# Order of a layer's superblocks, start of the output layer's weight tiles, start of a weight conversion, and the padding of the slots, in a three-layer kernel on one core

## The chip, the cores and the metric

The kernel runs on one core of a Trainium2 chip. The metric is the device time of one execution in microseconds (us); lower is better. The engines are TensorE (PE; PEld is its weight load), VectorE (DVE), ScalarE (ACT), GpSimd (POOL) and SyncE (SP). GpSimd and SyncE also issue DMAs: GpSimd's go through the software queue (q0), SyncE's through the hardware queue (q1).

## What is computed

```python
x = chunk_attention(q, k, v)          # (8, 8, 576, 64), softmax within chunks of 64 positions
x = x.transpose(0, 2, 1, 3).reshape(4608, 512)
h = x @ w_in                          # 512 x 2048
g = np.where(h > 0, h, np.exp(np.minimum(h, 0)) - 1)
y = g @ w_out                         # 2048 x 512
gate = 1 / (1 + np.exp(-(y @ w_gate)))  # 512 x 1536
out = (gate * (y @ w_val)) @ w_out2   # 1536 x 512, result 4608 x 512
```

The weights come as 64-bit floating-point words, which the kernel itself turns into pairs of a high and a low part.

## The kernel before

**Arithmetic.** Every factor is split into a high and a low part, and every product is three matmul passes (`PASSES`: high by high, low by high, high by low). The second layer, the gate and value layer and the output layer each replace the 8 block products of a 2x2 block product by 7, with sums on VectorE before and after (`PRODUCTS`, the order in which the four PSUM banks x, w, y, z take the 7 products).

**Stages on TensorE.** Stage 1 (0 to 504 us) is the attention (L463, L505) and the first layer (L395). Stage 2 (504 to 853 us) is the second layer (L721): five superblocks of token columns, four of 512 columns per half ("wide") and one, number 4, of 256 ("narrow"). The tuple `ORDER` (L51) says in which order they run. One superblock is 7 products of 48 matmuls. Stage 3 (853 to 1399 us) is the gate and value layer (L859, `unit`): 30 units `n`, six for each superblock in the order 0 to 4, so that units 24 to 29 are narrow; a unit is 7 products of 12 matmuls. Stage 4 (1399 to 1679 us) is the output layer (L990): 9 groups of 7 products of 36 matmuls.

**Weight tiles.** Converted weights lie in DRAM, in tiles of 0.5 MB (`wd_mid` for the second layer, `wd_glu` for gate and value, `wd_out` for the output). A pool `w` of 28 slots holds them in SBUF, together with the split operands of the products (`four`) and the tiles that a conversion works on. `hold(at, room, ahead)` (L320 to L339) is called after each product. It looks up the next `ahead` tiles from place `at` in the list `uses`, fetches those that are not held (L337, a DMA that GpSimd issues), and gives up the tiles used last if more than `room` are held. `uses` (L314 to L317) is the list of all products' tiles in order of time. A superblock of stage 2 uses 28 tiles; `room` is 20 without a conversion running and 12 with one, so that more or fewer tiles survive from one superblock to the next. Group 0 of stage 4 needs 21 `wd_out` tiles, three for each product, and the later groups use the same 21. GpSimd issues in program order: a load that waits for its slot holds up what stands behind it.

**Conversions.** `convert_pairs` (L196) loads raw words (`craw`, L209), puts its steps on ScalarE and VectorE in a list `todo`, from which `bg(n)` runs `n`, and stores the result (L290). The gate and value weights are converted in stage 2 (set up at L838), the output weights in stage 3 (set up at L1041; their raw words are loaded on SyncE's queue).

**Results of a unit.** A unit sums in `s` and `t` (two of ten 8 KB slots: `get`, `free`; a freed slot is given to the next `get` in order of freeing). ScalarE's sigmoids are L876, its first copy from PSUM is L878. `finish` (L912) multiplies gate by value (L914, L916) and stores the halves to DRAM (`gv<-s` L915, `gv<-t` L917, both on SyncE), then frees the slots. It runs after the second product of the next unit. For unit 28 (every sixth less two) the two multiplications are on GpSimd, so they stand in the same instruction stream as the weight loads. Four loads `c<-gv` (L934) bring the first group of stage 4 back; they stand on SyncE among the stores of units 25 to 28. SyncE issues in program order as well.

**Slots.** The ten 8 KB slots lie on two sides of SBUF, 6 right and 4 left. On the right side a tile `pad` (L87) of 8 words (32 bytes per partition) lies ahead of the pools of the right side. With it the right slots, the tiles `three` and stage 1's `x_r` start 64 bytes past a multiple of 128, while the left slots and the `w` pool start on multiples of 128. Where a slot holds `xc` (stage 3's first three operands) or `gc` (24 of the 36 weights of each product of stage 4), TensorE reads it.

Of the kernel before, what the change touches and what calls it, by code (L numbers as in the profile page):

```python
# [8 lines left out]
F32 = mybir.dt.float32  # L9
# [38 lines left out]
NLS = (512, 512, 512, 512, 256)  # L48
NJ = len(NLS)
START = tuple(2 * sum(NLS[:j]) for j in range(NJ))  # L50
ORDER = (0, 1, 2, 4, 3)  # L51
QU = F2 // 2
QM = F1 // 4
PAIRS_1, PAIRS_2 = 17, HF + 2 * QU
# [6 lines left out]
def kernel(  # L61
# [22 lines left out]
    x_l = pa.enter_context(tc.tile_pool(name="x_l", bufs=1))  # L84
    e_p = pa.enter_context(tc.tile_pool(name="e", bufs=4))
    pad_p = ctx.enter_context(tc.tile_pool(name="pad", bufs=1, side="right"))
    pad_p.tile([128, 8], F32, name="pad")  # L87
    pb = ExitStack()
    x_r = pb.enter_context(tc.tile_pool(name="x_r", bufs=1, side="right"))
    ps_p = ctx.enter_context(tc.tile_pool(name="ps", bufs=1, space=bass.MemoryType.PSUM))  # L90
# [15 lines left out]
    todo = []  # L106
# [206 lines left out]
    uses = [("mid", r, i) for _ in range(NJ) for i in range(7) for r in range(QM)]  # L313
    MID = len(uses)  # L314
    seq = [(j, q if j % 2 == 0 else QU - 1 - q) for j in range(NJ) for q in range(QU)]
    uses += [("glu", q, i) for _, q in seq for i in range(7)]
    uses += [("out2", r, i) for i in range(7) for r in range(QU // 2)]  # L317
    held = {}

    def hold(at, room, ahead):  # L320

        soon = {}
        for n, k in enumerate(uses[at:]):
            soon.setdefault(k, n)
        for k in list(held):
            if k not in soon:
                del held[k]
        need = list(soon)[:min(ahead, room)]
        for k in need:
            if not made(k):  # L330
                break
            if k not in held:
                while len(held) >= room:
                    del held[max(held, key=soon.get)]
                m, q, i = k
                t = held[k] = w_p.tile([128, 2, 2, 256], F32R, tag="w", name="w")
                nc.gpsimd.dma_start(out=t, in_=wd[m][q][:, (RIGHT if m == "out2" else LEFT)[i]])  # L337
        while len(held) > room:
            del held[max(held, key=soon.get)]  # L339
# [298 lines left out]
    def room(*busy):  # L638
        return NW - sum(busy)
# [44 lines left out]
    def stage_2(one):  # L684
# [137 lines left out]
        for o, j in enumerate(ORDER):  # L822
            nxt = ORDER[o + 1] if o + 1 < NJ else None
            for i in range(7):
                for p in range(QM):
                    product(j, i, p)
                    if o == i == p == 0:
                        one(end, False)
                        pa.close()
                        open_slots("left", 4)  # L830
                        three_p = ctx.enter_context(
                            tc.tile_pool(name="three", bufs=3, side="right", reuse_waits="tile")
                        )
                    beside(j, nxt, i, p)
                    if nxt is None:
                        for f in first_x.get((i, p), ()):
                            f()
                    if (o, i, p) == (1, 0, 0):  # L838
                        hold(7 * QM, room(8, 8), 10)
                        convert_pairs(range(PAIRS_1, PAIRS_2), nc.gpsimd)  # L840
                    if i in (2, 3, 5) and p > 0 and o > 0:
                        bg(2)
                    last = nxt is None and i >= 4
                    hold((7 * o + i) * QM + p + 1, room(8, 8 if todo or last else 0), 10)
                after(j, i)
# [4 lines left out]
    def unit(n):  # L850
        j, q = seq[n]
        last, third = n % QU == QU - 1, n % QU == QU - 3
        for i, c in enumerate(PRODUCTS):
            ps = bank[c][:, :, 0:NLS[j]]
            w = held["glu", q, i]
            for b in range(2):
                for k in range(2):
                    for p, (zw, zx) in enumerate(PASSES):
                        nc.tensor.matmul(  # L859
                            out=ps[:, b],  # L860
                            lhsT=w[:, b, zw, 128 * k:128 * k + 128],
                            rhs=x_part(j, i, zx, k),
                            start=(i < 4 and k == 0 and p == 0),
                            stop=(k == 1 and p == 2),
                            skip_group_check=True,
                        )
            if last:
                drop_x(j, i)
            parts = 8 if n + 1 < len(seq) else 2 * (7 - max(i, XC - 1))
            hold(MID + 7 * n + i + 1, room(parts, 9 if todo else 0), 14 if n < len(seq) - 3 else 22)  # L870
            if i == 0:
                s, t = get("s", (2, 2, NLS[j])), get("t", (2, 2, NLS[j]))
                u, v, c12 = s[:, 0], s[:, 1], t[:, 0]

                def sigmoid(x, of=None):
                    nc.scalar.activation(out=x, in_=x if of is None else of, func=ACTF.Sigmoid)  # L876

                nc.scalar.copy(out=u, in_=ps)  # L878
            elif i == 1:
                add(u, ps, u)  # L880
                while pending:
                    pending.pop(0)()
            elif i == 2:
                add(v, ps, u)
            elif i == 3:
                add(v, ps, v)
                sigmoid(v[:, 0])
            elif i == 4:
                sigmoid(t[:, 1, 0], ps[:, 0])
                nc.vector.tensor_tensor(out=t[:, 1, 0], in0=ps[:, 1], in1=t[:, 1, 0], op=ALU.mult)  # L890
            elif i == 5:
                add(c12, ps, u)
                sigmoid(c12[:, 0])
            else:
                add(u, ps, u)
                sigmoid(u[:, 0])
            if not last and not third:
                bg(1)
            if j + 1 < NJ:
                if n % QU == 1 and i >= 5:  # L900
                    load_x(j + 1, i - 5)
                if third and 1 <= i <= 3:
                    sum_x(j + 1, i)
                if last:
                    if i == 5:
                        sum_x(j + 1, 4)
                    split_x(j + 1, i)
                    if i == 6:
                        done_x(j + 1)
            yield  # L910

        def finish():  # L912
            eng = nc.gpsimd if n % QU == QU - 2 else nc.vector
            eng.tensor_tensor(out=s[:, :, 0], in0=s[:, :, 1], in1=s[:, :, 0], op=ALU.mult)  # L914
            nc.sync.dma_start(out=gvd[j][:, 0:2, q], in_=s[:, :, 0])  # L915
            eng.tensor_tensor(out=c12[:, 0], in0=c12[:, 1], in1=c12[:, 0], op=ALU.mult)  # L916
            nc.sync.dma_start(out=gvd[j][:, 2:4, q], in_=t[:, :, 0])  # L917
            free(s)
            free(t)
        pending.append(finish)  # L920

    def stages_3_4():
# [77 lines left out]
        def after(g, i):  # L1000
            if i == 0:
                ut[g] = four(2, 256)
                ot[g] = [four(2, DM) for h in range(2)]
            u, (lo, hi) = ut[g], ot[g]
            left, right = slice(0, 256), slice(256, 512)

            def store(h):
                j, k = groups[g]
                for n in range(2):
                    r = START[j] + h * NLS[j] + 256 * k + 128 * n  # L1010
                    nc.sync.dma_start(out=out[r:r + 128, :], in_=ot[g][h][:, n])

            if i == 0:
                nc.scalar.copy(out=u, in_=po["x"])
            elif i == 1:
                add(u, po["w"], u)
            elif i == 2:
                add(hi[:, :, right], po["y"], u)
            elif i == 3:
                add(hi[:, :, right], po["z"], hi[:, :, right])  # L1020
            elif i == 4:
                nc.scalar.copy(out=lo[:, :, left], in_=po["x"])
            elif i == 5:
                add(lo[:, :, right], po["y"], u)
                store(0)
            else:
                add(hi[:, :, left], po["z"], u)
                store(1)
                del ut[g], ot[g]

        N = len(seq)
# [6 lines left out]
            (N - 1, 5): lambda: split_g(0, 0, "c11", keep=True),  # L1038
        }
        for n in range(N):  # L1040
            if n == 2:  # L1041
                hold(MID + 7 * n, room(8, 9), 11)
                convert_pairs(range(PAIRS_2, len(tiles_of)), nc.sync)
            for i, _ in enumerate(unit(n)):
                beside.get((n, i), lambda: None)()
        for g in range(G):
            for i in range(7):
                prepare(g, i)
                product(g, i)
                after(g, i)  # L1050
                while pending:
                    pending.pop(0)()

# [63 lines left out]
```

## Time and profile before

| | us |
|---|---|
| runs shown, median of 3 | 1682.78 |
| lowest and highest of them | 1680.6, 1683.73 |
| the profiled execution, its own time | 1680.64 |
| its span, first to last instruction | 1678.9 |
| PE busy in the span | 1624.6 (97%) |
| DVE busy | 1205.5 (72%) |
| ACT busy | 752.4 (45%) |
| POOL busy | 308.9 (18%) |
| mean granted clock of TensorE | 0.991 of full speed |

A span is the profiled execution of one core; 1.7 us of the execution's time lie around it. In the rows below, "a<-b" is an operation that writes tile a from tile b, "xN" a count, and "<- X" names what ended a wait. A chain is the path that ended last in a stretch, piece by piece.

### The profile page before, as it was taken

What the parts mean: (1) busy time and instruction counts of PE and PEld (TensorE: products, weight loads), DVE (VectorE), ACT (ScalarE), POOL (GpSimd) and SP (SyncE); (2) the same over time, 40 slices, a digit from 0 to 9 for tenths busy, and PEclk for the clock granted to TensorE, in tenths of its full rate; (3) what the DMA queues carried; (4) which work ended last, traced back from release to release, by engine and by line L of the source; (5) the groups of instructions that cost most, each with busy time, mean ns of one, the idle gap of its engine ahead of it and who ended that gap; (6) DMA issues with size and microseconds to landing.
All of it is one profiled execution on the core that took longest, in us unless ns stands there. A gap on an engine that the chain in (4) does not pass through costs nothing.

```text
span 1678.9 us, 27430 instructions
## 1 busy us (share of the span) xinstructions
PE 1624.6 (97%) x10644; PEld 1385.7 (83%) x10644; DVE 1205.5 (72%) x1703; ACT 752.4 (45%) x1277; POOL 308.9 (18%) x502
## 2 busy tenths in 40 slices
PE   6899999999999999999999999999999977999998
PEld 4677777777788888898887888888888977999998
DVE  7878888888547898877945676766744626777776
ACT  5766767666544465545512332422312213333342
POOL 3421122211101122221121222222220230000000
PEclk9999999999999999999999999999999998999999
DMA  6679889898789799998799679699492696443431
GB/s 223 201 238 295 279 286 296 293 293 280 259 290 320 268 301 378 300 362 293 210 322 316 198 248 390 201 342 334 128 403 90 236 390 201 145 158 113 157 132 51
DMA packets 178433, 429.10 MB, mean 256 GB/s; under 512 B 14208, under 2 KB 55168, under 8 KB 173184
## 3 DMA queue, kind: packets, MB, share of 16 engines
q0 software_dynamic: 73344, 223.90, 40.3%
q1 hardware_dynamic: 104960, 203.45, 35.3%
q8 instruction: 84, 1.38, 0.3%
q14 instruction: 45, 0.37, 0.1%
HBM read 294.65 MB, written 132.64 MB: 255 GB/s over the span
## 4 chain that ended last, share of the span: by engine, by line
PE 72%; DVE 12%; ACT 6%; DMA 6%; issue 2%; SPq 1%; POOL 0%; ACTq 0%; DVEq 0%; POOLq 0%
PE bank_x L859 8%; PE bank_y L859 8%; PE bank_z L859 8%; PE bank_y L721 6%; PE bank_z L721 6%; PE bank_x L721 6%; PE bank_x L990 5%; PE bank_z L990 4%; PE bank_w L859 4%; PE bank_y L395 4%; PE bank_w L395 3%; PE bank_z L395 3%; PE bank_w L721 3%; PE bank_y L990 3%; PE bank_w L990 2%
## 5 line engine op out<-in xcount | busy, mean ns | idle before, releaser
L95 ACT CAST four<-b 128x512 fp32r<-128x512 f32 (+1 forms) x240 | 129.1, 576 | 81.4 <-PE bank_y L721 30.9
L101 DVE TENSOR_TENSOR four<-b,four 128x512 fp32r<-128x512 f32 (+1 forms) x240 | 141.3, 632 | 33.3 <-ACT four L95 32.5
L859 PE MATMUL bank_z<-four,w 128*128 128x512 f32 (+1 forms) x720 | 158.5, 369 | 0.0
L876 ACT ACTIVATE s<-s 128x512 f32<-128x512 f32 (+1 forms) x60 | 35.4, 590 | 250.4 <-DVE s L104 250.4
L859 PEld LDWEIGHTS bank_z<-four,w 128*128 128x128 f32 x720 | 126.3, 189 | 23.4
L395 PE MATMUL bank_w<-xs,w 128*128 128x512 f32 x576 | 141.0, 399 | 0.0
L395 PE MATMUL bank_y<-xs,w 128*128 128x512 f32 x576 | 138.9, 395 | 1.4 <-POOL w L167 0.9
L337 POOL DMA_DIRECT2D w<-wd_glu x172 | 92.7, 543 | 255.9 <-PE bank_x L859 68.6
L395 PE MATMUL bank_z<-xs,w 128*128 128x512 f32 x576 | 138.9, 396 | 0.0
L395 PEld LDWEIGHTS bank_y<-xs,w 128*128 128x128 f32 x576 | 106.5, 188 | 23.6 <-POOL w L167 1.2
L395 PEld LDWEIGHTS bank_w<-xs,w 128*128 128x128 f32 x576 | 107.2, 190 | 22.2
L395 PEld LDWEIGHTS bank_z<-xs,w 128*128 128x128 f32 x576 | 107.2, 189 | 22.2
L721 PE MATMUL bank_y<-four,w 128*128 128x512 f32 (+1 forms) x480 | 100.7, 368 | 3.2 <-DMA w<-wd_mid 2.6
L337 POOL DMA_DIRECT2D w<-wd_mid x102 | 54.4, 537 | 267.1 <-DVE four L101 58.2
L721 PE MATMUL bank_x<-four,w 128*128 128x512 f32 (+1 forms) x480 | 100.2, 368 | 0.0
L721 PE MATMUL bank_z<-four,w 128*128 128x512 f32 (+1 forms) x480 | 100.2, 368 | 0.0
L721 PEld LDWEIGHTS bank_y<-four,w 128*128 128x128 f32 x480 | 83.8, 188 | 18.6 <-issue 2.5
L721 PEld LDWEIGHTS bank_x<-four,w 128*128 128x128 f32 x480 | 83.8, 189 | 15.0
L721 PEld LDWEIGHTS bank_z<-four,w 128*128 128x128 f32 x480 | 83.8, 189 | 14.9
L104 DVE TENSOR_TENSOR s<-bank_z,s 128x1024 f32<-128x1024 f32 (+1 forms) x60 | 66.9, 1115 | 37.6 <-PE bank_z L859 37.2
L104 DVE TENSOR_TENSOR s<-bank_w,s 128x1024 f32<-128x1024 f32 (+1 forms) x30 | 33.5, 1116 | 83.9 <-PE bank_w L859 45.3
L859 PE MATMUL bank_x<-four,w 128*128 128x512 f32 (+1 forms) x360 | 80.1, 373 | 10.3 <-ACT s L878 10.3
(165 smaller groups left out, 3321.4 us busy)
## 6 DMA issues: line engine op xcount, KB each, us to landing
w<-wd_glu POOLq DMA_DIRECT2D x172, 512.0 KB, 8.6
w<-wd_mid POOLq DMA_DIRECT2D x102, 512.0 KB, 6.9
gd<-elu SPq DMA_DIRECT2D x72, 512.0 KB, 3.8
b<-gd SPq DMA_DIRECT2D x32, 1024.0 KB, 9.0
c<-gv SPq DMA_DIRECT2D x36, 768.0 KB, 5.2
wd_glu<-ch POOLq DMA_DIRECT2D x36, 512.0 KB, 4.8
raw<-in_qkv SPq DMA_DIRECT2D x61, 256.0 KB, 3.9
wd_mid<-ch POOLq DMA_DIRECT2D x24, 512.0 KB, 5.0
```

The costliest lines, as they stand in the source:

```text
L95: nc.scalar.copy(out=out, in_=raw)
L101: lo_eng.tensor_sub(out=lo, in0=raw, in1=hi)
L104: nc.vector.tensor_tensor(out=out, in0=a, in1=b, op=ALU.add)
L337: nc.gpsimd.dma_start(out=t, in_=wd[m][q][:, (RIGHT if m == "out2" else LEFT)[i]])
L395: nc.tensor.matmul(out=h_bank(d)[:, n], lhsT=w[:, zw, kk * 128:(kk + 1) * 128], rhs=xs[j, kk][:, zx], start=(kk == 0 and p == 0), stop=(kk ...
L721: nc.tensor.matmul(out=bank[PRODUCTS[i]][:, u, 0:NLS[j]], lhsT=w[:, k, zw, 128 * u:128 * u + 128], rhs=t[:, zx], start=(i < 4 and p == 0 a ...
L859: nc.tensor.matmul(out=ps[:, b], lhsT=w[:, b, zw, 128 * k:128 * k + 128], rhs=x_part(j, i, zx, k), start=(i < 4 and k == 0 and p == 0), st ...
L876: nc.scalar.activation(out=x, in_=x if of is None else of, func=ACTF.Sigmoid)
L990: nc.tensor.matmul(out=po[c][:, m], lhsT=t[:, zx, q % 4, 128 * m:128 * m + 128], rhs=w[:, q % 2, zw], start=(i < 4 and q == 0 and p == 0 a ...
```

## The change

The edits are all in the order or place of work; the arithmetic is untouched.

```diff
-ORDER = (0, 1, 2, 4, 3)
+ORDER = (0, 4, 1, 2, 3)
...
-    pad_p.tile([128, 8], F32, name="pad")
+    pad_p.tile([128, 24], F32, name="pad")
...
-    uses += [("out2", r, i) for i in range(7) for r in range(QU // 2)]
+    uses += 2 * [("out2", r, i) for i in range(7) for r in range(QU // 2)]
...
-                    if (o, i, p) == (1, 0, 0):
-                        hold(7 * QM, room(8, 8), 10)
+                    if (o, i, p) == (2, 0, 0):
+                        hold(14 * QM, room(8, 8), 10)
                         convert_pairs(range(PAIRS_1, PAIRS_2), nc.gpsimd)
-                    if i in (2, 3, 5) and p > 0 and o > 0:
+                    if i in (2, 3, 5) and p > 0 and o > 1:
                         bg(2)
...
-            hold(MID + 7 * n + i + 1, room(parts, 9 if todo else 0), 14 if n < len(seq) - 3 else 22)
+            hold(MID + 7 * n + i + 1, room(parts, 9 if todo else 0), 14 if n < len(seq) - QU else 10)
...
-            if not last and not third:
+            if not last and not third and n > 1:
                 bg(1)
...
-            if n == 2:
+            if n == 1:
                 hold(MID + 7 * n, room(8, 9), 11)
                 convert_pairs(range(PAIRS_2, len(tiles_of)), nc.sync)
...
                 after(g, i)
+                if g == 0:
+                    hold(MID + 7 * N + 3 * (i + 1), room(7), 10 if i < 4 else 21)
```

Stage 2's narrow superblock runs second instead of fourth, and the conversion of the gate and value weights, which stood beside superblocks 1 and 2, stands beside the same two in their new places. On TensorE this is the only difference (`bank_x` to `bank_z` are the four PSUM banks):

```order
 L721 MATMUL bank_z<-four,w 128x512 x48
+L721 MATMUL bank_x<-four,w 128x256 x48
+L721 MATMUL bank_w<-four,w 128x256 x48
+L721 MATMUL bank_y<-four,w 128x256 x48
+L721 MATMUL bank_z<-four,w 128x256 x48
+L721 MATMUL bank_x<-four,w 128x256 x48
```

These are the first five of the seven narrow products (256 columns), now right behind the first wide superblock; the same seven rows are gone between the fourth and the fifth superblock of the other order.

On SyncE at the start of stage 3, `craw<-in_w_out` are the first raw words of the output's weights, `gv` the stores of a unit and `x` the loads of the next superblock's operand:

```order
 L738 DMA ymid_69<-u 128x1024
+L209 DMA craw<-in_w_out 128x1024 x2
 L915 DMA gv_71<-s 128x2x512
 L917 DMA gv_71<-t 128x2x512
 L646 DMA x<-ymid_67 128x1024 x4
-L209 DMA craw<-in_w_out 128x1024 x2
 L915 DMA gv_71<-s 128x2x512
```

The two raw loads moved from behind unit 0's stores and the four loads of `x` to ahead of them.

On GpSimd at the end of stage 3, `w<-wd_out` are the output's weight tiles (three DRAM tensors in turn), L914 and L916 the multiplications of unit 28. First before, then the change:

```order
L337 DMA w<-wd_out_88 128x1024
L337 DMA w<-wd_out_86 128x1024 x2
L914 TENSOR_TENSOR s<-s 128x2x256
L916 TENSOR_TENSOR t<-t 128x256
L337 DMA w<-wd_out_87 128x1024
```

```order
L337 DMA w<-wd_glu_85 128x1024 x7
L337 DMA w<-wd_out_86 128x1024
L337 DMA w<-wd_out_87 128x1024
L337 DMA w<-wd_out_88 128x1024
L337 DMA w<-wd_out_86 128x1024
L337 DMA w<-wd_out_87 128x1024
L914 TENSOR_TENSOR s<-s 128x2x256
L916 TENSOR_TENSOR t<-t 128x256
L337 DMA w<-wd_out_88 128x1024
```

Before, 14 loads of output tiles stood ahead of the multiplications and 8 behind; now 5 stand ahead and 16 behind. In all there are 21 loads of `wd_out` where there were 22 (one was given up and loaded again), 172 of `wd_glu` as before, and 105 of `wd_mid` where there were 102.

The larger pad moves the tiles of the right side by 64 bytes: the right slots, `three` and `x_r` now start on multiples of 128 bytes, and the attention's tiles of stage 1 on the right side (`raw`, `vals`, `ident` and their like) start 64 bytes past one, where they started on a multiple.

## Rows read from the trace of the kernel before

**Rows 1.** PE's waits, 700 to 1679 us: line and releaser, us, times, longest.
```profile
PE bank_x L859 <- ACT s L878: 10.3, 1, 10.3
PE bank_x L859 <- DVE t L890: 7.1, 1, 7.1
PE bank_y L721 <- DMA w<-wd_mid: 2.6, 2, 2.3
PE bank_y L859 <- DVE s L104: 2.5, 1, 2.5
```

**Rows 2.** Engines' busy time in one stretch; last three: granted clock, DMA share, GB/s.
```profile
1330.00:1366.00 36.00, 35.92 (x301) 35.71 (x299) 15.80 (x28) 7.09 (x16) 12.16 (x23) 1.00 1.12 393
```

**Rows 3.** The chain that ended last, 1360 to 1420 us: start, us, piece.
```profile
1355.30 19.94 DMA gv<-t
...
1375.75 14.63 DMA gv<-s
...
1390.48 0.59 ACT s L878
...
1400.15 5.60 PE bank_x L990 x32
```

**Rows 4.** Timeline of SP's queue, 1330 to 1396 us: start, us, issue.
```profile
1354.26 0.36 SPq L934 DMA_DIRECT2D c<-gv  x1
...
1375.29 0.36 SPq L934 DMA_DIRECT2D c<-gv  x1
```

**Rows 5.** Timeline of POOL, 1345 to 1396 us; in brackets the idle time before.
```profile
1356.57 0.53 POOL L337 DMA_DIRECT2D w<-wd_out  x1 [1.17 <-DMA w<-wd_glu]
...
1369.81 0.53 POOL L337 DMA_DIRECT2D w<-wd_out  x1 [1.18 <-DMA w<-wd_out]
1376.80 1.29 POOL L914 TENSOR_TENSOR s<-s 128x512 f32<-128x512 f32 x1
```

**Rows 6.** Timeline of ACT and PE there: the two late starts.
```profile
1372.13 0.38 ACT L876 ACTIVATE t<-bank_x 128x256 f32<-128x256 f32 x1 [9.35 <-DMA gv<-s]
...
1391.12 2.93 PE L859 MATMUL bank_x<-four,w 128*128 128x256 f32 x12 [10.34 <-ACT s L878]
...
1395.39 1.60 PE L859 MATMUL bank_z<-four,w 128*128 128x256 f32 x12
```

**Rows 7.** DMA issues, 1300 to 1440 us: count, KB each, median us to landing.
```profile
w<-wd_out POOLq DMA_DIRECT2D x22, 512.0 KB, 11.6
...
gv<-s SPq DMA_DIRECT2D x2, 512.0 KB, 4.7
```

**Rows 8.** The chain, 725 to 790 us: the narrow superblock of stage 2.
```profile
732.30 5.75 PE bank_x L721 x48
...
751.32 16.13 DMA w<-wd_mid
...
776.45 10.91 PE bank_x L721 x48
```

**Rows 9.** DMA issues beside stage 2's first superblock, 504 to 580 us.
```profile
w<-wd_mid POOLq DMA_DIRECT2D x16, 512.0 KB, 6.3
```

**Rows 10.** The chain, 880 to 930 us: the raw words, and one wide unit from 912.92.
```profile
884.81 16.28 DMA craw<-in_w_out
...
912.92 2.76 PE bank_x L859 x12
915.68 2.75 PE bank_w L859 x12
918.43 2.77 PE bank_y L859 x12
921.20 2.72 PE bank_z L859 x12
```

**Rows 11.** The chain, 1398 to 1679 us: two products of stage 4.
```profile
1418.89 4.27 PE bank_x L990 x36
...
1449.20 4.32 PE bank_x L990 x36
```

## The prediction

> **What bounds the kernel now.** I read the page first: TensorE is busy 97% of the span, so time can be won only where it waits or where its own instructions get shorter. Second, the list of TensorE's waits [rows 1]: behind the start-up there are four places worth naming, and together they are 22.5 us. The reader is to see that two of them, 10.3 and 7.1 us, are single waits on ScalarE and VectorE in the gate and value layer, 2.6 us is a wait for a weight tile in stage 2, and 2.5 us a wait on a sum in stage 3. Third, I followed each back in the chain of waits. The two long ones stand at the end of stage 3, and neither engine is slow there: ScalarE's step at 1372.13 sat idle 9.35 us for a store `gv<-s` [rows 6], and its L878 at 1390.48 stands behind another that took 14.63 us [rows 3]. So **the end of stage 3 is bound by stores of a quarter megabyte that do not land.** The slots of units 26 and 27 are given out again only when these stores have landed. Fourth, the view of stretches tells why: from 1330 to 1366 the DMA engines are at a share of 1.12 and move 393 GB/s [rows 2]. GpSimd issues an output weight tile about every 1.66 us there (nine from 1356.57 to 1369.81) [rows 5]. The hardware queue gets little beside that: a `c` load, a store of `s` and one of `t`, 1.31 MB in all, go from 1354.26 [rows 4] to 1375.24 (1355.30 + 19.94) [rows 3], which is 63 GB/s.
>
> **The change part by part.** The sum is made against the profiled execution's own 1680.64 us, which is 2.1 us under the median of the runs, 1682.78.
>
> *Output weight tiles.* Before, 14 of these loads stood on GpSimd ahead of unit 28's two multiplications, now 5. The fifth is the one issued at 1356.57 [rows 5]; up to it the stream is the same, and each load waits for the same slots, so nothing is won before. Then GpSimd stands at the multiplication until unit 28's sigmoid is done, which before was at 1376.80 [rows 5]. The loads already issued, at most eight, drain in 8 x 1.66 = 13 us, until about 1369.5. By then the hardware queue has moved 15.2 us x 63 GB/s = 0.96 of its 1.31 MB. The rest, 0.35 MB, goes alone; a store of 512 KB with little beside it took 4.7 us [rows 7], so about 2 us, and `t` of unit 26 lands near 1371.3 instead of 1375.24. SyncE then issues the next `c` load and the store of unit 27, as it did at 1375.29 [rows 4], 4 us sooner. These two are 1 MB, twice the 512 KB, so between 4.7 and 9.4 us; I take the middle, 7.1, against 14.63. L878 then runs near 1379.0 instead of 1390.48 [rows 3]. What follows it, 9.7 us to the output's first long run at 1400.15 [rows 3], is work of ScalarE and VectorE and stays. **Term: -11.5.** Ends: nothing, if both stores land as late as before; and -22, if both waits go (17.4), with the slow products behind them (2.93 us for twelve matmuls after the wait, 1.60 two products later [rows 6]; the granted clock is down after TensorE has stood idle) and the short waits at the output's start. I stay in the middle since unit 26's store still shares the engines until 1369.5.
>
> What moves behind: 16 tiles are now issued from about 1377 on. At 1.66 us each the last is issued near 1402 and lands some 5 us after its data has its turn, by 1407. The group would start near 1388, uses three tiles in each product of about 4.3 us [rows 11], and needs the last three at 1388 + 6 x 4.3 = 1414. I cost it at nothing; if that cover is gone, see the second rival. The one load fewer counts for nothing, as TensorE does not wait there.
>
> *Narrow superblock second.* It took 776.45 - 732.30 = 44.15 us [rows 8], and seven products of 5.76 are 40.3: 3.8 lost. The chain shows a weight tile of 16.13 us, issued at 751.32 [rows 8]. As fourth, the narrow superblock came behind a conversion, when only 12 tiles could be held, and had to fetch most of its 28 at half a wide superblock's time per product. As second, it follows a superblock without a conversion: 20 tiles are held, 8 are missing, and they are asked for in its first two products, ten products ahead, 14.4 us. Loads beside the first superblock took 6.3 us in the median [rows 9]. What is late next would be the tiles of the wide superblock behind it: the first of them is asked for twelve narrow products ahead, about 16 us, when the next operand's 1 MB loads are on the way, and even the worst load above, 16.13, costs only tenths there. **Term: -3.8**, ends 0 and -3.8. The conversion beside superblocks 1 and 2 moves with them: nothing, since the same steps stand beside the same products. The three more loads of 0.5 MB are hidden, as TensorE's waits in stage 2 are only these.
>
> *Raw words a unit earlier.* The pair issued behind the stores and `x` loads took 16.28 us [rows 10], and the conversion steps that waited for it, in order on ScalarE and VectorE, held up a sum, for which TensorE waited 2.5 us [rows 1]. Now the pair is issued some 25 us earlier, ahead of the stores. At the same 16.28 it has landed before its first step. **Term: -2.5**, ends 0 and -2.7 (the unit's whole excess). What it pushes back on SyncE, the store of unit 0, has a unit of 19 us to land.
>
> *Pad.* It takes no instruction away. In a wide unit the three products that read `xc`, mostly in right slots, take 2.76, 2.75 and 2.77 us and the others 2.72 [rows 10]: 0.12 us a unit, over 24 wide units 2.9 us, which goes if the slot's place is the cause. In stage 4 the same product takes 4.27 or 4.32 us [rows 11]; by the slots that the program gives out, the 34 of 63 that read `gc` 64 bytes past a multiple of 128 are the shorter ones, so with all of them on a multiple 34 x 0.05 = 1.7 us are added. The two signs are as the rows give them. Stage 1, where attention tiles move the other way: no row here tells; some 64 slots at the same 0.05 give ends of +3 and -3, and I take nothing. **Term: -1.2**, ends +4.7 and -5.9.
>
> The Trainium skill, page "SBUF — State Buffer", section "Who interferes with whom", says that TensorE never waits on anyone for SBUF, and its section "Operand start alignment" asks only for a multiple of the element size, as a matter of legality and not of speed. By it the pad is worth nothing and the sum is 1.2 us higher. The two durations above speak against it; no run here shows that the address is their cause.
>
> **Sum:** -11.5 - 3.8 - 2.5 - 1.2 = -19.0, so 1680.64 - 19.0 = **1661.6 us**.
>
> **The rivals.** *The stores stay slow.* The late store of unit 27 was issued at 1375.75 [rows 3], when GpSimd's tile loads had paused since 1369.81 [rows 5], and still took 14.63. That speaks for a queue that is slow for its own reasons, or for a backlog longer than I drained. Then only the 4 us of the earlier issue remain: 1680.64 - 4.0 - 3.8 - 2.5 - 1.2 = 1669.1. Against it: tiles in flight from before the pause, and the loads that GpSimd resumed, explain a good part.
>
> *Output tiles too late (slower).* Sixteen tiles, 8 MB, now come while group 0 runs, beside the `c` loads of group 1 and the first output stores. It decides from the point where a tile takes more than (1414 - 1382)/15 = 2.1 us, counted from the first landing near 1382. Each 1 us more per tile then adds 15 us of waiting. At 4 us a tile, 131 GB/s, this is 28 us, and the kernel comes to 1661.6 + 28 = 1690. For it: 63 GB/s is what the other queue got in a crowd [rows 3, 4]. Against it: the software queue itself kept 1.66 us through the worst crowd [rows 5].
>
> *The pad does nothing*, the page's case above: the pace is a matter of something else, such as which operand is read. The sum is then 1662.8.
>
> *The change does not do what it says.* Ten tiles ahead is not less than what was issued in time for the first five, and the stall goes on as it was; with the narrow superblock's wait turning up at the wide one behind it, 1680.64 - 2.5 = 1678.1, no difference that can be told.
>
> **How the numbers follow.** Chances: forecast 0.55, slow stores 0.22, pad without effect 0.15, tiles too late 0.04, nothing moved 0.04. About 0.2%, 3.4 us, is what a measurement of this kernel can tell from no change. The first three are all faster by more: 0.92; same 0.04; slower 0.04. The range goes down to 1653, where a further 4 us of the waits and 4.7 of the pad's lower end go too, and up to 1673, the slow stores with the narrow superblock's loss kept.
>
> **What would show it.** In the changed profile: `gv<-s` of unit 27 near 7 us, the wait on ACT L878 down from 10.3 to a few us, and the one on DVE L890 to about 5; no wait of L721 for `w<-wd_mid`; no wait of `bank_y` L859 on the sum near 907; all products of stage 4 at 4.32 and all of a wide unit at 2.72. The forecast is wrong if L990 waits for `w<-wd_out`, if the stores still take 14 us, or if a new wait stands at the second superblock of stage 2.

## The result and the profile after

The changed kernel takes 1663.83 us in the median of 5 runs (1663.11 to 1666.58), against 1682.78 us before: a ratio of 0.9898 with a 95% interval of [0.9882, 0.9915], some 19 us less. The forecast was 1661.6 us. The profiled execution after is the longest of the five, 1666.58 us (span 1664.8); a second profiled execution of the same kernel, 1663.93 us (span 1662.2), is shown beside it. TensorE is busy 1623.2 us of the first span, 97%, against 1624.6 before; so of the 14.1 us by which the span is shorter, 12.7 are idle time of TensorE.

TensorE's time, read from the first matmul of each superblock, unit and group in its timeline:

| stretch (us) | before | after | after, again |
|---|---|---|---|
| stage 1, to the first L721 | 503.66 | 505.94 | 505.46 |
| stage 2 | 348.82 | 344.98 | 344.98 |
| stage 3, units 0 to 23 | 463.11 | 456.96 | 456.96 |
| units 24 to 27 | 40.14 | 40.31 | 40.31 |
| units 28 and 29 | 43.16 | 29.75 | 28.49 |
| stage 4, group 0 | 32.64 | 38.06 | 37.16 |
| groups 1 to 8 | 242.98 | 244.45 | 244.46 |
| rest | 4.36 | 4.36 | 4.35 |

Stage 1 is the part that the change hardly touches. Over the 14 profiles of this study it ends anywhere from 503.3 to 507.0 us, with either pad, so its 2 us here are taken as the spread of single executions.

TensorE's waits after, 180 to 1679 us, in the columns of [rows 1]:

```profile
PE bank_x L859 <- DVE t L890: 4.8, 1, 4.8
PE bank_z L990 <- ACT gc L95: 4.4, 1, 4.4
PE bank_x L990 <- ACT gc L95: 2.3, 1, 2.3
PE bank_x L505 <- DVE p L499: 1.0, 6, 0.2
```

The 10.3 us on L878, the 2.6 on weight tiles and the 2.5 on the sum of [rows 1] are gone, the 7.1 is 4.8, and two waits are new: 4.4 us in the output's group 0, and 1.0 us in six small pieces in stage 1 (L505). The 2.3 us at the output's start were 1.9 before.

The chain of the changed kernel from 600 to 705 us, the end of the narrow superblock, as [rows 8]:

```profile
616.82 5.76 PE bank_z L721 x48
622.58 10.91 PE bank_x L721 x48
```

TensorE goes from product to product. From 866 to 912 us, unit 1, as [rows 10]:

```profile
870.12 2.72 PE bank_x L859 x12
872.84 2.72 PE bank_w L859 x12
875.56 2.72 PE bank_y L859 x12
878.28 2.72 PE bank_z L859 x12
```

There is neither the wait for raw words nor a product over 2.72 us. In stage 4, as [rows 11], the products of groups 1 to 8 are the longer kind, but for the fourth of each group, which takes 4.6 us (4.5 to 4.7 before), and the last:

```profile
1433.74 4.32 PE bank_x L990 x36
1438.06 4.32 PE bank_y L990 x36
```

At the end of stage 3, GpSimd's timeline, as [rows 5]:

```profile
1348.48 0.53 POOL L337 DMA_DIRECT2D w<-wd_out  x1 [1.19 <-PE bank_z L859]
1365.07 1.28 POOL L914 TENSOR_TENSOR s<-s 128x512 f32<-128x512 f32 x1 [16.07 <-ACT s L876]
1366.32 0.72 POOL L916 TENSOR_TENSOR t<-t 128x256 f32<-128x256 f32 x1
1366.99 4.30 POOL L337 DMA_DIRECT2D w<-wd_out  x8
```

Behind the fifth output tile GpSimd stands for 16 us, then eight tiles go out at once. ScalarE's timeline there, as [rows 6]:

```profile
1362.31 0.38 ACT L876 ACTIVATE t<-bank_x 128x256 f32<-128x256 f32 x1 [7.01 <-DMA gv<-s]
...
1369.53 0.59 ACT L878 COPY s<-bank_x 128x512 f32<-128x512 f32 x1 [4.54 <-DMA gv<-s]
...
1395.21 1.04 ACT L95 CAST gc<-c 128x1024 fp32r<-128x1024 f32 x1 [9.82 <-DMA gv<-t]
```

L878 runs 7.2 us behind the late L876, where it was 18.4 us before (1390.48 less 1372.13). The store it waits for, issued at 1363.39, is the only one of the stretch 1363 to 1366 us among the DMA issues, as [rows 7]:

```profile
gv<-s SPq DMA_DIRECT2D x1, 256.0 KB, 6.0
```

It took 6.0 us where [rows 3] has 14.63. The third row belongs to the new wait. The chain shows its store, which is unit 29's:

```profile
1384.67 10.46 DMA gv<-t
...
1395.21 1.05 ACT gc L95
...
1396.31 1.23 PE bank_z L990 x4
```

and the view of stretches, as [rows 2], what it met:

```profile
1366.00:1402.00 36.00, 28.43 (x208) 27.32 (x208) 21.34 (x24) 10.11 (x16) 9.52 (x18) 0.89 1.11 382
```

The DMA engines are full again, at 382 GB/s, now while unit 29 ends and group 0 runs. The granted clock in this stretch is 0.89 of full speed; it fell to the lower of its two levels, 1.2 GHz, in the new wait, and stayed there for 6.8 us from 1394.2.

### The profile page after: what moved, and what is told of

Its sections match the earlier page's. It is cut to its first block, busy times and chain, and to the rows that moved or that the text cites. A ratio compares the mean times of both kernels' runs of the same rounds, so it can differ in the third digit from the quotient of the medians.

```text
span 1664.8 us, 27426 instructions
## 1 busy us (share of the span) xinstructions
PE 1623.2 (97%) x10644; PEld 1388.2 (83%) x10644; DVE 1202.8 (72%) x1703; ACT 750.5 (45%) x1277; POOL 310.6 (19%) x504
## 4 chain that ended last, share of the span: by engine, by line
PE 71%; DVE 14%; ACT 8%; issue 3%; DMA 3%; POOL 0%; SPq 0%; ACTq 0%; DVEq 0%; POOLq 0%
PE bank_x L859 8%; PE bank_z L859 8%; PE bank_y L859 8%; PE bank_x L721 6%; PE bank_z L721 6%; PE bank_y L721 6%; PE bank_z L990 5%; PE bank_x L990 4%; PE bank_w L859 4%; PE bank_w L721 3%; PE bank_y L990 3%; DVE elu L418 2%; PE bank_y L395 2%; PE bank_z L395 2%; PE bank_w L990 2%
## 5 line engine op out<-in xcount | busy, mean ns | idle before, releaser
L101 DVE TENSOR_TENSOR four<-b,four 128x512 fp32r<-128x512 f32 (+1 forms) x240 | 140.1, 633 | 33.5 <-ACT four L95 33.3
L876 ACT ACTIVATE s<-s 128x512 f32<-128x512 f32 (+1 forms) x60 | 35.4, 590 | 251.1 <-DVE s L104 251.1
L395 PEld LDWEIGHTS bank_w<-xs,w 128*128 128x128 f32 x576 | 107.0, 190 | 21.7
L721 PE MATMUL bank_x<-four,w 128*128 128x512 f32 (+1 forms) x480 | 100.2, 368 | 0.0
L721 PE MATMUL bank_y<-four,w 128*128 128x512 f32 (+1 forms) x480 | 100.2, 368 | 0.0
L721 PE MATMUL bank_z<-four,w 128*128 128x512 f32 (+1 forms) x480 | 100.2, 368 | 0.0
L721 PEld LDWEIGHTS bank_x<-four,w 128*128 128x128 f32 x480 | 83.7, 189 | 15.0
L721 PEld LDWEIGHTS bank_y<-four,w 128*128 128x128 f32 x480 | 83.7, 189 | 15.0
L721 PEld LDWEIGHTS bank_z<-four,w 128*128 128x128 f32 x480 | 83.7, 189 | 15.0
L104 DVE TENSOR_TENSOR s<-bank_w,s 128x1024 f32<-128x1024 f32 (+1 forms) x30 | 33.5, 1116 | 71.7 <-PE bank_w L859 44.7
L859 PE MATMUL bank_x<-xc,w 128*128 128x512 f32 (+1 forms) x360 | 79.9, 372 | 4.8 <-DVE t L890 4.8
```

The source lines that it names most:

```text
L101: lo_eng.tensor_sub(out=lo, in0=raw, in1=hi)
L104: nc.vector.tensor_tensor(out=out, in0=a, in1=b, op=ALU.add)
L395: nc.tensor.matmul(out=h_bank(d)[:, n], lhsT=w[:, zw, kk * 128:(kk + 1) * 128], rhs=xs[j, kk][:, zx], start=(kk == 0 and p == 0), stop=(kk ...
L721: nc.tensor.matmul(out=bank[PRODUCTS[i]][:, u, 0:NLS[j]], lhsT=w[:, k, zw, 128 * u:128 * u + 128], rhs=t[:, zx], start=(i < 4 and p == 0 a ...
L859: nc.tensor.matmul(out=ps[:, b], lhsT=w[:, b, zw, 128 * k:128 * k + 128], rhs=x_part(j, i, zx, k), start=(i < 4 and k == 0 and p == 0), st ...
```

## The experiments

All ratios are against the kernel before, run on the same chip; its medians there were 1678.38 to 1680.18 us. A ratio is not the quotient of the two medians; the two differ by up to 0.14% here.

**Each part alone.** The pad alone:

```diff
-    pad_p.tile([128, 8], F32, name="pad")
+    pad_p.tile([128, 24], F32, name="pad")
```

> The kernel before with the pad of 24 words alone. Theory (the place in SBUF sets TensorE's pace): in stage 3 every wide unit is 0.14 us shorter, 24 of them 3.4 us; in stage 4 all products take 4.32 us, some 1.7 us more; stage 1 moves by at most 3 us either way; the waits at the end of stage 3 stay. In all 1 to 3 us faster than before. Rival (the place does nothing, the changed kernel's shorter units come from elsewhere): wide units stay at 19.19 us and products of stage 4 at 4.27 and 4.32, the time is the one before.

Ratio 0.9993 [0.9984, 1.0002] over 12 runs, 1679.51 us: the time alone can't tell it from nothing. The profile can: every wide unit but the one with the raw words' wait takes 19.04 us instead of 19.16 to 19.19, groups 1 to 7 of stage 4 take 30.54 or 30.55 instead of 30.2 to 30.5. So the pad, by where it puts the tiles of the right side, does set TensorE's pace, with both signs: -3.4 us in the wide units, +1.5 in stage 4. One small wait appears in stage 1, among its waits:

```profile
PE bank_x L505 <- DVE p L499: 1.1, 6, 0.2
```

It stands in every profile with the pad of 24 words (1.0 or 1.1 us) and in none with 8 or 40.

The order alone, with the conversion one superblock later as in the change:

```diff
-ORDER = (0, 1, 2, 4, 3)
+ORDER = (0, 4, 1, 2, 3)
...
-                    if (o, i, p) == (1, 0, 0):
-                        hold(7 * QM, room(8, 8), 10)
+                    if (o, i, p) == (2, 0, 0):
+                        hold(14 * QM, room(8, 8), 10)
...
-                    if i in (2, 3, 5) and p > 0 and o > 0:
+                    if i in (2, 3, 5) and p > 0 and o > 1:
```

> The kernel before with the narrow superblock second, and the conversion moved with superblocks 1 and 2. Theory (the narrow superblock waited for weight tiles because only 12 were held): it takes 40.3 us instead of 44.1, stage 2 is 3.8 us shorter, and nothing else moves: 3 to 5 us faster. Rival (the wait only moves on): a wait of 2 us or more at the wide superblock behind it, and no gain.

Ratio 0.9978 [0.9968, 0.9987], 3.7 us. The narrow superblock takes 40.31 us (44.14 before), the four wide ones 76.2 as ever, and TensorE waits nowhere in stage 2. The wait did not move on.

The raw words alone:

```diff
-            if not last and not third:
+            if not last and not third and n > 1:
...
-            if n == 2:
+            if n == 1:
```

> The kernel before with the output weights' raw words set up in unit 1 and no conversion step before unit 2. Theory (the step that waited for the raw words held up a sum): unit 2 takes 19.2 us instead of 22.0, the wait of bank_y L859 on the sum is gone, 2.5 to 2.8 us faster. Rival (the sum waits for something else, or the pair lands as late): unit 2 stays at 22 us, or unit 1 becomes longer.

Ratio 0.9972 [0.9956, 0.9989], which is 4.7 us; the medians, 1677.35 and 1679.68, are 2.3 us apart, with 1671.58 to 1679.78 over 6 runs. Unit 2 takes 19.16 instead of 21.96, 2.8 us less, and unit 1 is not longer; the interval holds that. What unit 2 loses without this part is not the same in every kernel: 1.8 to 2.8 us in the three other profiles with the narrow superblock fourth, and 4.0 us in the run of the order alone.

The output tiles alone (the doubled list, 10 ahead in the narrow units, the loads in group 0; the second of the three edits is shown):

```diff
...
-            hold(MID + 7 * n + i + 1, room(parts, 9 if todo else 0), 14 if n < len(seq) - 3 else 22)
+            hold(MID + 7 * n + i + 1, room(parts, 9 if todo else 0), 14 if n < len(seq) - QU else 10)
...
```

> The kernel before with the output tiles' part alone: the list of uses twice, 10 tiles ahead in the narrow units, and the loads in group 0. Theory (14 loads ahead of unit 28's multiplications crowded the stores out): units 28 and 29 together take some 30 us instead of 43, a wait of 4 to 5 us for a slot stands in group 0, and the net is 8 to 9 us faster. Rival (part of that gain needs the pad or the other order, or group 0's wait comes from the pad): the two units stay above 36 us, or group 0 has no wait.

Ratio 0.9958 [0.9942, 0.9974], 7.1 us. Its waits:

```profile
PE bank_x L859 <- DVE t L890: 4.4, 1, 4.4
...
PE bank_z L990 <- ACT gc L95: 2.8, 1, 2.8
```

Units 28 and 29 take 29.25 us, group 0 takes 38.12: the same gain and the same new wait as in the whole change, without the other three parts; the wait is under the 4 to 5 us expected in this execution, and the time some 1 us short of it. The four parts alone add up to 0.07 + 0.22 + 0.28 + 0.42 = 0.99%, the whole change gave 1.02%. With intervals of 0.1 to 0.2% on each part, that shows no interaction larger than some 0.3%; it does not show that there is none.

**What frees the stores.** Unit 28's multiplications on VectorE, so that GpSimd has nothing to stand at:

```diff
-            eng = nc.gpsimd if n % QU == QU - 2 else nc.vector
+            eng = nc.gpsimd if n % QU == QU - 2 and n < len(seq) - QU else nc.vector
```

> The changed kernel with unit 28's two multiplications on VectorE, so that nothing on GpSimd stands between the fifth output tile and the others. Theory (the gain at the end of stage 3 comes from GpSimd standing at the multiplications, which keeps tile loads off the DMA engines for some 15 us): GpSimd's loads go on every 1.4 to 1.8 us behind the fifth, the store of unit 27 takes 12 us or more again, units 28 and 29 take 36 to 43 us instead of 29.8, and group 0 has less than 2 us of waiting: 3 to 9 us slower than the changed kernel. Rival (the gain comes from asking for 10 tiles instead of 22): no slower than the changed kernel.

Ratio 0.9936 [0.9921, 0.9951]: 0.3 to 0.4% slower than the changed kernel, 4 to 6 us. GpSimd issues ten output tiles, not five, and stops there, since the next slot is still in use:

```profile
1354.68 0.53 POOL L337 DMA_DIRECT2D w<-wd_out  x1 [1.15 <-DMA w<-wd_out]
1367.48 0.53 POOL L337 DMA_DIRECT2D w<-wd_out  x1 [12.27 <-PE bank_x L859]
```

The chain shows which store pays:

```profile
1346.24 20.24 DMA gv<-t
...
1366.99 5.73 DMA gv<-s
```

Unit 26's `t` takes 20.24 us, as before (19.94, [rows 3]); unit 27's `s`, for which 12 us or more were expected, takes 5.73, since by then the tiles have stopped. Units 28 and 29 come to 38.1 us, between 43.2 and 29. A wait of 5.2 us stands right ahead of group 0, behind unit 28's own `s` (7.05 us in the chain). The theory is right about the net and about the crowd, wrong about which store. The rival has a share, but a small one, and its size is open: units 28 and 29 and group 0 together take 71.3 us here, against 75.8 in the kernel before and 72.4 to 74.4 in the other four profiles with the output tiles as before, so 1 to 4.5 us of the gain come without the multiplications on GpSimd. By the ratios it is about 1 us (0.64% here, 0.57% for the order, the raw words and the pad alone). The whole change takes 67.8 or 65.7 us there.

One store shows what the crowd costs. Unit 29's `t` is issued here when the last tile has landed, and takes 2.5 us, as it did in the kernel before; in every profile in which the tiles are still under way it takes 10.0 to 10.5. Among the DMA issues from 1391.5 to 1391.9 us:

```profile
gv<-t SPq DMA_DIRECT2D x1, 256.0 KB, 2.5
```

**The new wait in group 0.** Unit 29's multiplication and stores, ahead of the first group instead of behind its first product:

```diff
+        while pending:
+            pending.pop(0)()
         for g in range(G):
```

> The changed kernel with unit 29's multiplication and stores ahead of the splits for the output's second product, instead of behind the first product. Theory (group 0's wait of 4.4 us is for the slot of unit 29's t, whose store was issued at 1384.7 and took 10.5 us): the stores are issued 3 to 4 us sooner, the wait of bank_z L990 falls to 1 us or less, up to 1.5 us is lost at the start of the output; 2 to 4 us faster than the changed kernel. Rival (the store is slow because 16 tiles are under way, whenever it is issued): it lands no sooner and nothing is won.

Ratio 0.9880 [0.9864, 0.9897], 1658.64 us; beside the changed kernel's 0.9898 and 0.9910 that is 3 to 5 us less. SyncE's timeline has the stores 5.1 us sooner (1384.26 in the changed kernel); 2.3 us of it is that this execution came to group 0 sooner, so the edit moved them by 2.7 us, a little less than expected:

```profile
1379.20 0.36 SPq L915 DMA_DIRECT2D gv<-s  x1
```

The wait of `bank_z` is gone, group 0 takes 32.45 us, and no longer wait stands at the output's start (2.3 us as before it). So group 0 waited for unit 29's stores, not for tiles. The stores are no faster, as the rival has it: `t` takes 10.46 us again, with the tiles under way as before. It only lands early enough.

**Fewer tiles ahead.** On top of that, 7 or 5 instead of 10 ahead in units 28 and 29:

```diff
-            hold(MID + 7 * n + i + 1, room(parts, 9 if todo else 0), 14 if n < len(seq) - QU else 10)
+            hold(MID + 7 * n + i + 1, room(parts, 9 if todo else 0), 14 if n < len(seq) - QU else 10 if n < len(seq) - 2 else 7)
```

> The kernel with unit 29's stores early, and 7 instead of 10 tiles ahead in units 28 and 29, so that 2 output tiles instead of 5 stand ahead of unit 28's multiplications. Theory (each tile ahead of them puts 1.3 to 1.7 us between the stores of units 25 and 26 and their landing): the first wait, 3.8 us, falls to 1 us or less, while the tiles for the output's first products come as late as they are needed; 1 to 3 us faster than with unit 29's stores early alone. Rival (the tiles become the bound): waits of L990 for w<-wd_out as long as what is won.

Ratio 0.9854 [0.9836, 0.9871], **1654.94 us, the best kernel of this study**: 25 us under the kernel before and 9 under the changed one, which ran beside it at 1663.93. By the ratios it is 4.4 us under the kernel with unit 29's stores early alone, more than the 1 to 3 expected. Its waits, 700 to 1660 us:

```profile
PE bank_x L990 <- ACT gc L95: 2.3, 1, 2.3
PE bank_z L859 <- DVE s L104: 0.6, 1, 0.6
PE bank_x L859 <- ACT s L878: 0.5, 1, 0.5
PE bank_x L990 <- DVE gc L101: 0.5, 1, 0.5
```

The first wait is gone, and no wait is for a tile. Group 0 still takes 34.11 us, since its first product runs at the clock's lower level (6.8 us from 1370.8) and takes 7.9 us. With 5 ahead:

```diff
-... 14 if n < len(seq) - QU else 10 if n < len(seq) - 2 else 7)
+... 14 if n < len(seq) - QU else 10 if n < len(seq) - 2 else 5)
```

> The same with 5 ahead in units 28 and 29: no output tile ahead of unit 28's multiplications. Theory: the first wait is gone or under 1 us, and the output's first product waits for its tiles by 0 to 3 us; within 2 us of 7 ahead. Rival: all 21 tiles behind the multiplications make group 0 wait by 5 us or more, slower than with 10 ahead.

Ratio 0.9869 [0.9851, 0.9887], 1656.59 us. Units 28 and 29 are down to 21.7 us (24.3 with 7 ahead), but group 0 takes 35.4 (34.1), and group 1 now 33.5 instead of 30.5:

```profile
PE bank_x L990 <- ACT gc L95: 4.8, 2, 3.4
```

A second wait on the split of the output's operands, not on tiles, takes back what was won. The chain has a load of group 1 in front of it, and the products behind it run at the clock's lower level (6.8 us from 1402.1), which is the longer group 1:

```profile
1382.85 18.79 DMA c<-gv
```

So the crowd now meets group 1's `c` loads. The time is within 2 us of 7 ahead.

**What the narrow superblock lacked.** Narrow second, but the conversion beside it: the order's edit without the second one.

```diff
-ORDER = (0, 1, 2, 4, 3)
+ORDER = (0, 4, 1, 2, 3)
```

> The kernel before with the narrow superblock second, but the conversion starting beside it as the second superblock, not one later. Theory (what the narrow superblock lacked is room, 12 tiles held beside a conversion instead of 20): it has to fetch most of its tiles and takes 44 us or more, so that at least the 3.8 us come back. Rival (it lacked nothing but an idle DMA stretch, and second place alone gives it): it takes 40.3 us as without the conversion.

Ratio 1.0093 [1.0078, 1.0108], 1694.52 us. The narrow superblock takes 57.1 us, and TensorE waits:

```profile
PE bank_y L721 <- DMA w<-wd_mid: 4.3, 3, 2.1
PE bank_z L721 <- DMA w<-wd_mid: 3.6, 2, 2.1
PE bank_y L721 <- ACT four L95: 2.6, 1, 2.6
```

With the conversion beside it second place gains nothing, so that rival falls. Most of the 11.7 us of waits are for tiles, as the theory has it (8.7); but the conversion's own work on ScalarE and VectorE holds up splits too (3.0), and what each is worth was not separated. Of the other 5 us of the 16.8 lost, some 3.7 are work at the clock's lower level: it fell for 10.2 us from 621.1, after the waits had begun, and TensorE was busy 7.4 us of these at half speed.

**The pad's place.** The changed kernel with 40 words: the remainder by 128 bytes of the kernel before, 128 bytes further on.

```diff
-    pad_p.tile([128, 24], F32, name="pad")
+    pad_p.tile([128, 40], F32, name="pad")
```

> The changed kernel with a pad of 40 words, so that the right slots lie 64 bytes past a multiple of 128 again, but 128 bytes from where the kernel before had them. Theory (the start within 128 bytes sets TensorE's pace): wide units 19.16 to 19.19 us, groups of stage 4 30.2 to 30.45 us as in the kernel before. Rival (which region of SBUF or how far the slots lie from other tiles): 19.04 and 30.54 as in the changed kernel. In time 1 to 3 us slower than the changed kernel by the theory.

Ratio 0.9943 [0.9928, 0.9958], 1669.17 us. Two rows of its chains, a product with `xc` and one of stage 4 with `gc`:

```profile
908.90 2.80 PE bank_x L859 x12
```

```profile
1451.01 4.16 PE bank_x L990 x36
```

The wide units are long again (19.22 to 19.30 us) and the groups of stage 4 short (29.8 to 30.3). The remainder by 128 gives the sign, as the theory has it; it does not give the size, which is larger than in the kernel before (2.76 and 4.27) on both sides. The wide units cost 5.8 us more than in the changed kernel, groups 1 to 8 cost 3.2 less and units 24 to 27 0.5 less: 2.1 us net. The medians stand 5 us or more apart, though they were not taken on the same chip; where the other 3 lie stays open.

With unit 29's stores early, the pad of 8 words once more:

```diff
-    pad_p.tile([128, 24], F32, name="pad")
+    pad_p.tile([128, 8], F32, name="pad")
```

> The kernel with unit 29's stores early and the pad of 8 words of the kernel before. Theory (the place sets the pace, with both signs): wide units 19.16 to 19.3 us, 3 to 6 us more over 24; groups of stage 4 shorter by 1.5 to 3.3 us in all; net 1 to 3 us slower than with the pad of 24. Rival (stage 1 pays for the pad of 24): no slower, or faster.

Ratio 0.9884 [0.9866, 0.9902], against 0.9880 with 24 words: no difference that can be told. By stages, the wide units cost 3.4 us more, groups 1 to 8 cost 1.5 less and group 0 costs 1.2 less, net some 0.5 with units 24 to 27. The signs are the theory's, the net is under its 1 us.

**The changed kernel again**, unedited:

> The changed kernel itself, once more, beside the three below: a second profiled execution and its time on the chip on which they run. Theory (executions of one kernel differ mostly in stage 1): units, superblocks and groups 1 to 8 of stage 4 are as in the first profile to 0.1 us, and only the start of stage 2 (503 to 507 us in all profiles so far) and the waits at the end of stage 3 move; 0.989 to 0.991 of before. Rival: the waits at the end of stage 3 and in group 0 differ by several us from one execution to the next.

Ratio 0.9910 [0.9895, 0.9924], 1663.93 us. The third column of the table is this run: superblocks, units 0 to 27 and groups 1 to 8 agree to 0.02 us. What moves is stage 1 (0.5), units 28 and 29 (1.3) and group 0 (0.9), where the two waits are 3.9 and 2.6 us instead of 4.8 and 4.4:

```profile
PE bank_x L859 <- DVE t L890: 3.9, 1, 3.9
PE bank_z L990 <- ACT gc L95: 2.6, 1, 2.6
```

## Why the prediction held, point by point

The forecast was 1661.6 us, the median is 1663.83. The difference was 19.0 us, forecast and measured (1682.78 less 1663.83), but from two starting points: the forecast starts at one execution of 1680.64, against which the two profiles after are 14.1 and 16.7 us shorter (stage 1 alone is 2 us longer in them), and the second comparison gave 16.3 us (1680.18 less 1663.93).

*Narrow superblock second: -3.8 forecast, -3.84 measured*, in the change and alone; in three other profiles with it fourth it takes 44.6 to 44.8 us, so -4.3 to -4.5. Nothing came late behind it, as argued, though the cover was worked out short (twelve products of 1.44 us are 17 us, not 16). That room for tiles was the reason is supported, not settled, since the conversion beside it brings work of its own.

*Raw words a unit earlier: -2.5 forecast, -2.8 measured.* The whole excess of unit 2 went. How large it is without this part varies from one profile to the next, 1.8 to 4.3 us in the five without it.

*Output weight tiles: -11.5 forecast; -13.4 and -14.7 in units 28 and 29, but +5.4 and +4.5 in group 0, so -8.0 and -10.2.* The cause was read rightly: GpSimd stands at the multiplications (16 us), unit 26's `t` takes 15.1 us instead of 19.94 (4.8 less, forecast 4), the store of unit 27 lands after 6.0 us (forecast 7.1), the first wait is 4.8 and 3.9 (forecast about 5), the second is gone, and L990 never waits for a tile. The rival of slow stores falls with the 6.0. One step was worked out too short: 0.35 MB at the pace of a 512 KB store in 4.7 us are 3.2 us, not 2. **The step that failed is the cost of what moves behind:** "I cost it at nothing". I looked only at whether the 16 tiles come in time, and they do. But they fill the DMA engines (382 GB/s from 1366 to 1402) while unit 29's stores are on their way (10.46 us for `t`, where 2.5 were enough without tiles), and a slot that group 0 needs comes free only when these have landed. It is the very mechanism that the first part of the prediction had found for units 26 and 27, now at unit 29. The early store shows it: 2.7 us sooner against group 0, and the wait is gone. Also too simple was that the multiplications alone do it: without them on GpSimd 1 to 4.5 us of the gain remain; that this is because only ten tiles, not 14, go out before the slots run short was not tested by itself.

The one execution that the term was read from was also a costly one. Units 28 and 29 and group 0 take 75.8 us in it, and 72.4 to 74.4 in the four other profiles with the tiles as before (unit 27's `s` takes 10.5 to 14.6 us in the five), so the net gain lies between 4.6 and 10.2 us by whichever profiles are compared; the run of the part alone gave 7.1. Nor is a wait the whole price: around the waits there the clock was at its lower level for 20.5 us in the kernel before and for 10.2 and 13.7 us in the changed one.

*Pad: -1.2 forecast.* By stages -3.4 in the wide units (forecast -2.9, read from a unit of the first superblock; from unit 6 on four products are longer, not three, 0.15 us a unit), +1.5 in groups 1 to 8 (+1.7 in all of stage 4), +0.2 in the narrow units (left out): -1.7. Its time alone, -0.07%, can't be told from nothing, nor can its removal from the faster kernel. The rival that the pad does nothing falls: the same twelve matmuls take 2.72, 2.76 or 2.80 us by the pad. By the Trainium skill, page "SBUF — State Buffer", section "Who interferes with whom", TensorE never waits on anyone for SBUF. These durations do not contradict that sentence, since no run shows a wait on another engine in them; it does not cover them.

That the difference came out to 0.05 us is luck: the end of stage 3 gave 1.3 to 3.5 us less than its term and the others 0.8 more, and the median before, 1682.78, is 2.6 to 4.4 us above the medians of the same kernel in the three later comparisons.

## What to carry to other kernels

A store whose slot somebody waits for is as much on the path as a load: find what fills the DMA engines between its issue and its landing, and hold that back or issue the store earlier. Work held back goes somewhere, so ask which store or load it meets there; here two lines, unit 29's stores early and three tiles fewer ahead, gave another 9 us on top of the change. When a change has several parts, run each alone and read the stages: parts of 3 us that the time could hardly tell stood out in the profile, to hundredths where TensorE does not wait. Where it waits, one profile is not enough: the same wait differs by 1 to 4 us from one to the next.

## What was not expected

TensorE's pace depends on where the tiles of the right side lie, and not in one direction. With `xc` as the moving operand (the one that streams through the weights), 64 bytes past a multiple of 128 is slower (2.76 or 2.80 against 2.72 us in the wide units); with `gc` as the stationary operand (the weights) it is faster (4.27 or 4.16 against 4.32). In the narrow units even the moving operand is faster there: 10.03 (pad of 8) and 9.92 (40) us a unit against 10.08 (24). Two places with the same remainder by 128 differ (pads of 8 and 40 words), so there is more to it than that remainder. Nor is it the operand's own start alone: in units 6 to 23 the first product behind the three with `xc` reads `four`, which no pad moves, and takes 2.77 (pad of 8) or 2.74 us (40) instead of 2.72. No run here says why.
